# Centring the first row tile on ScalarE, and a 128-column tile of zeros for the warm-up products

## The chip, the cores and the metric

The kernel runs on one core of a Trainium2 chip. The metric is the device time of one execution in microseconds (us); five executions give a median. The profile shows one execution of its own, from the first to the last instruction (the span). Engines are named as the profile names them: PE is TensorE, PEld its weight loads, DVE is VectorE, ACT is ScalarE, POOL is GpSimd, and SP is the engine that issues most of the DMAs.

## The reference

S = 2048 tokens, D = 512 features, F = 1792; everything is bfloat16.

```python
def _layernorm(x, axis=-1, eps=1e-5):
    m = jnp.mean(x, axis=axis, keepdims=True)
    v = jnp.var(x, axis=axis, keepdims=True)
    return (x - m) / jnp.sqrt(v + eps)

def reference(x, w1, w2, w3, w4):
    h = _gelu(_layernorm(x, axis=-1) @ w1)
    # four quarters of the features of h are shifted along S by +1, -1, +2, -2 tokens
    hs = jnp.concatenate([g0, g1, g2, g3], axis=-1) @ w2
    x1 = x + hs
    h2 = _gelu(_layernorm(x1, axis=-1) @ w3) @ w4
    return x1 + h2
```

## The kernel before

The tokens are cut into 16 row tiles of 128 tokens. In layer 1 a tile is normalised in rows (tokens on partitions), transposed to features on partitions (`xnT`), multiplied with w1 and passed through gelu into `hT` ("up1"). "mix" multiplies the shifted `hT` with w2 and DVE adds x, which gives x1. Layer 2 normalises x1 (tile numbers q = 16 to 31), multiplies with w3 and applies gelu ("up2"), and "down" multiplies with w4; DVE adds x1 and the result is stored.

The order of the PE work is written out by hand in `SCRIPT`:

```python
warm:10 sa:0 sb:0 ty:1 ra:0 rb:0 ty:2 up1:1 th:0 up1:2 mix:0 ty:3 ty:5 mix:1 ty:4 up1:3-4 ty:16 mix:2 ty:17
```

`warm:10` is ten products of zeros. `sa`/`sb` are the transposes on PE of the left and the right half of tile 0 (two 128x128 transposes each, L487), and `ty:1` the four transposes of tile 1. `ra`/`rb` are the two halves of tile 0's product with w1 (two 128x512 products each, L525). Tile 0 alone (`NAT`, `SPLIT`) takes another way than the other tiles: it is only centred before its transpose, in two halves of 256 columns, its product comes out in rows, and the gelu (L566) multiplies with 1/std on the way, `rstd0`. `th:0` then turns its result (L591), and DVE copies it into `hT` (L601). Later tiles go through DMA transposes from SP.

All other instructions are placed by a planner (`Program.order`, `place`). It takes a guessed duration `dur` for each operation and a due time that comes from the PE order, runs a list schedule, and so fixes the order on each engine's queue. A changed duration or engine can therefore reorder other operations; the queues themselves run strictly in that order. `emit` puts waits where data demand them. The order of the loads is fixed by `LOADS`: SP issues x1, x2, w1a, w1b, x3, x4-5, w2a, w2b and so on, and ACT issues x0.

The steps of tile 0 that matter here are these. ACT computes the mean with `sum0`, a Copy whose accumulator goes to `mv` (L393), and the sum of squares with `ssq0` (L398). DVE makes the variance, `msq0` and `vpe0` (L406, L410). POOL raises it to the power -1/2 (`rstd0`, L421) and also centres the two halves (`norm0_0` and `norm0_1`, L432). After each transposed half, a copy out of PSUM brings it into `xnT` (L495): ACT does the left half (`ev0_0`) and DVE the right half (`ev0_1`). Tile 1's transposed half goes out in the same way, left by ACT (`ev1act`) and right by DVE (`ev1dve`).

Of the kernel before, what the change touches and what calls it, by code (L numbers as in the profile page):

```python
# [6 lines left out]
P = 128  # L7
ACT_F = mybir.ActivationFunctionType
# [249 lines left out]
        return out  # L258

GROUPS = {1: (1, 1, 1, 1, 2, 1, 4, 2, 2, 1), 2: (2, 4, 4, 2, 4)}  # L260
NORM = {0: "pool", 3: "act", 7: "pool", 8: "act", 9: "pool", 10: "pool", 11: "pool", 12: "pool", 14: "act", 15: "act", 16: "pool", 18: "act", 19: "act", 24: "pool", 25: "act", 26: "pool", 27: "pool", 29: "pool", 30: "pool", 31: "act"}
EVAC = {0: "both", 1: "both", 2: "both", 4: "both", 8: "both", 9: "dve", 10: "dve", 11: "dve", 12: "dve", 13: "dve", 14: "dve", 16: "dve", 17: "dve", 19: "both", 20: "both", 21: "both", 22: "both", 23: "both", 24: "dve", 25: "both", 27: "both", 29: "both", 30: "both", 31: "both"}
STAT_ACT = (0, 7, 9, 12, 13, 15, 18, 21, 25, 29, 30)
TAIL = (256, 128, 128)
# [16 lines left out]
def bass_standalone__mixer_s_mlp__prompt_kernel(nc, x, w1, w2, w3, w4, out):  # L281
# [14 lines left out]
    with ExitStack() as es:  # L296
# [21 lines left out]
        neghalf = sb("neghalf", [P, 1], F32)  # L318
        eps_c = sb("eps_c", [P, 1], F32)
        warm = sb("warm", [P, 1], F32)  # L320
        zeros = sb("zeros", [P, 512], BF16)
        y_ps = es.enter_context(nc.psum_tensor("y_ps", [P, NPAIR, 1024], F32))
        o_ps = es.enter_context(nc.psum_tensor("o_ps", [P, NOB, 512], F32))
        o_bf = o_ps[:, :, :].bitcast(BF16)
# [19 lines left out]


        def consts():
            pg.add("dve", "zeros", lambda e: e.memset(zeros[:], 0.0), writes=[(("zeros",), 0)], dur=300)
            pg.add("pool", "ident0", lambda e: e.memset(ident[:], 0.0), writes=[(("ident",), 0)], dur=200)
            pg.add("pool", "ident1",
                   lambda e: e.affine_select(out=ident[:], in_=ident[:], compare_op=ALU.not_equal, fill=1.0,  # L350
                                             base=0, pattern=[[-1, P]], channel_multiplier=1),
                   reads=[(("ident",), 0)], writes=[(("ident",), 1)], dur=300)
            pg.add("pool", "trip0", lambda e: e.memset(st9[:, :, 6:8], 0.0), writes=[(("trip", 0), 0)], dur=90)
            pg.add("pool", "trip1", lambda e: e.memset(st9[:, :, 8:9], D * LN_EPS), writes=[(("trip", 1), 0)], dur=80)
            pg.add("pool", "epsc", lambda e: e.memset(eps_c[:], LN_EPS), writes=[(("eps",), 0)], dur=70)
            pg.add("pool", "neghalf", lambda e: e.memset(neghalf[:], -0.5), writes=[(("neghalf",), 0)], dur=70)
            pg.add("pool", "pad0", lambda e: e.memset(hT[:, :, 0:2], 0.0), writes=[(("hpad", 0), 0)], dur=100)
            pg.add("pool", "pad1", lambda e: e.memset(hT[:, :, HTW - 2 : HTW], 0.0),
                   writes=[(("hpad", 1), 0)], dur=100)
# [24 lines left out]
        def ln(layer, t):  # L384
            q = t if layer == 1 else NT + t
            src = x_sb[:, t, :] if layer == 1 else x1_sb[:, t, :]
            rs = [(("x", t), 0)] if layer == 1 else [(("x1", t), 0)]
            col = lambda a: a[:, q : q + 1]
            if q in STAT_ACT:
                if layer == 1:  # L390
                    b, v = next_junk()
                    pg.add("act", f"sum{q}",
                           (lambda d: (lambda e: e.activation(d, src, ACT_F.Copy, scale=1.0 / D,  # L393
                                                              accum_out=mv[:, q, 0:1])))(junk[:, b, :]),
                           reads=rs, writes=[(("mv", q), 0), (("junk", b), v)], dur=610)
                b, v = next_junk()
                pg.add("act", f"ssq{q}",
                       (lambda d: (lambda e: e.activation(d, src, ACT_F.Square, accum_out=sums[:, q, 1:2])))(  # L398
                           junk[:, b, :]),
                       reads=rs, writes=[(("ssq", q), 0), (("junk", b), v)], dur=610)  # L400
                if layer == 2:
                    pg.add("dve", f"mean{q}",
                           lambda e: e.tensor_scalar(mv[:, q, 0:1], sums[:, q, 0:1], 1.0 / D, None, ALU.mult),
                           reads=[(("sum", q), 0)], writes=[(("mv", q), 0)], dur=75)
                pg.add("dve", f"msq{q}",
                       lambda e: e.tensor_scalar(mv[:, q, 1:2], mv[:, q, 0:1], mv[:, q, 0:1], LN_EPS, ALU.mult,  # L406
                                                 ALU.subtract),
                       reads=[(("mv", q), 0)], writes=[(("msq", q), 0)], dur=130)
                pg.add("dve", f"vpe{q}",
                       lambda e: e.scalar_tensor_tensor(col(vpe), sums[:, q, 1:2], 1.0 / D, mv[:, q, 1:2], ALU.mult,  # L410
                                                        ALU.subtract),
                       reads=[(("ssq", q), 0), (("msq", q), 0)], writes=[(("vpe", q), 0)], dur=130)
            else:
                pg.add("dve", f"bnst{q}", lambda e: e.bn_stats(st9[:, q, 0:6], src),  # L414
                       reads=rs, writes=[(("st", q), 0)], dur=605)
                pg.add("dve", f"bnag{q}", lambda e: e.bn_aggr(mv[:, q, :], st9[:, q, :]),  # L416
                       reads=[(("st", q), 0), (("trip", 0), 0), (("trip", 1), 0)],
                       writes=[(("mv", q), 0), (("vpe", q), 0)], dur=75)
# [1 line left out]
            pg.add("pool", f"rstd{q}",  # L420
                   lambda e: e.tensor_tensor(col(rstd), var, neghalf[:], ALU.pow),  # L421
                   reads=[(("vpe", q), 0), (("neghalf",), 0)], writes=[(("rstd", q), 0)], dur=470)
            how = NORM.get(q, "dve")
            dst = xn_buf[:, slot(q), :]
            if q in NAT:

                assert how != "act"
                if t in SPLIT:
                    for hh in (0, 1):
                        cs = slice(hh * D // 2, (hh + 1) * D // 2)  # L430
                        pg.add(how, f"norm{q}_{hh}",
                               (lambda a, b: (lambda e: e.tensor_scalar(a, b, mv[:, q, 0:1], None, ALU.subtract)))(  # L432
                                   dst[:, cs], src[:, cs]),
                               reads=rs + [(("mv", q), 0)], writes=[(("xn", slot(q), hh), q)],
                               dur=195 if how == "dve" else 400)
                    return
                pg.add(how, f"norm{q}",
                       lambda e: e.tensor_scalar(dst, src, mv[:, q, 0:1], None, ALU.subtract),
                       reads=rs + [(("mv", q), 0)], writes=[(("xn", slot(q), hh), q) for hh in (0, 1)], dur=330 if how == "dve" else 760)
            elif how == "dve":  # L440
                pg.add("dve", f"norm{q}",
                       lambda e: e.tensor_scalar(dst, src, mv[:, q, 0:1], rstd[:, q : q + 1], ALU.subtract, ALU.mult),  # L442
                       reads=rs + [(("mv", q), 0), (("rstd", q), 0)], writes=[(("xn", slot(q), hh), q) for hh in (0, 1)], dur=330)
            else:
                eng = NMR.get(q, "dve")
                pg.add(eng, f"nmr{q}",
                       lambda e: e.tensor_scalar(nmr[:, q : q + 1], mv[:, q, 0:1], rstd[:, q : q + 1], -1.0,  # L447
                                                 ALU.mult, ALU.mult),
                       reads=[(("mv", q), 0), (("rstd", q), 0)], writes=[(("nmr", q), 0)], dur=130 if eng == "dve" else 280)
                if how == "act":  # L450
                    f = lambda e: e.activation(dst, src, ACT_F.Identity, bias=nmr[:, q : q + 1],  # L451
                                               scale=rstd[:, q : q + 1])
                else:
                    f = lambda e: e.tensor_scalar(dst, src, rstd[:, q : q + 1], nmr[:, q : q + 1], ALU.mult, ALU.add)  # L454
                pg.add(how, f"norm{q}", f, reads=rs + [(("nmr", q), 0), (("rstd", q), 0)],
                       writes=[(("xn", slot(q), hh), q) for hh in (0, 1)], dur=710 if how == "act" else 760)
# [253 lines left out]

        def warm_pe(n):
            b, v = next_bank()

            def f(e):
                for _ in range(n):
                    ins = e.matmul(o_ps[:, b, :], zeros[:, 0:P], zeros[:], start=True, stop=True)  # L716
                return ins

            nwarm[0] += 1
            pg.add("pe", f"warm{nwarm[0]}", f, reads=[(("zeros",), 0)], writes=[(("o", b), v)],  # L720
                   dur=min(n, 7) * 427 + max(0, n - 7) * 216)
            next_bank()
# [145 lines left out]
```

## Time and profile before

| | us |
|---|---|
| median of 5 runs | 135.95 (135.87 to 136.23) |
| the profiled execution, whole | 135.9 |
| its span | 134.6 |
| PE busy in it | 130.8 (97%) |
| DVE, ACT, POOL busy | 50.4, 57.4, 31.5 |
| ten warm-up products on PE (L716), start and length | 0.63, 4.44 |
| POOL's two centring instructions (L432), start and length together | 3.76, 1.82 |

The 1.3 us between the span and the time lie before the first and after the last instruction. PE carries nearly the whole chain that ended last (94%), so a change of another engine's work counts only where PE waits. A line of the timeline gives the start and the length of a merged group in us, the engine (a q behind the name is its queue of DMA issues), the source line, the operation with the tiles out and in, and in brackets how long the engine was idle before and what ended that.

### The profile page before, as it was taken

The numbers are of one execution on the slowest core, as the hardware profiler recorded it, in microseconds if no ns is written. First come the engines' busy times: TensorE is split into PE (matmuls) and PEld (weight loads), VectorE is DVE, ScalarE is ACT, GpSimd is POOL, SyncE is SP. The second block draws the span as 40 slices with busy tenths as digits, with TensorE's granted clock in tenths as the row PEclk, the third lists the DMA queues.
The fourth block names the chain that finished last, engine by engine and source line by source line (L and its number), as shares of the span: only waits on it lengthen the run. The fifth ranks groups of instructions, "written<-read, shape, count | busy, mean of one in ns | idle before, by whom it ended". The sixth has DMA issues, their size and how long they took to land.

```text
span 134.6 us, 2004 instructions
## 1 busy us (share of the span) xinstructions
PE 130.8 (97%) x777; PEld 71.6 (53%) x790; DVE 50.4 (37%) x134; ACT 57.4 (43%) x90; POOL 31.5 (23%) x70
## 2 busy tenths in 40 slices
PE   8899999999999999999999999999999999999994
PEld 3377687644656444479444444444444444444463
DVE  4589976856178930070061004232222200012222
ACT  6379349989534275547315554000000155520000
POOL 3944548893102860006010001100000000000000
DMA  5999998645543134100311000211111100001112
GB/s 159 285 366 405 350 300 214 111 84 117 115 82 81 33 72 92 39 0 3 80 39 39 0 0 0 73 44 42 41 39 61 56 0 0 0 5 39 39 39 78
DMA packets 21289, 12.19 MB, mean 91 GB/s; under 512 B 13856, under 2 KB 20768, under 8 KB 21280
## 3 DMA queue, kind: packets, MB, share of 16 engines
q1 hardware_dynamic: 20704, 11.80, 33.1%
q10 hardware_dynamic: 576, 0.26, 0.7%
q8 instruction: 6, 0.10, 0.3%
q14 instruction: 3, 0.02, 0.1%
HBM read 6.82 MB, written 2.10 MB: 66 GB/s over the span
## 4 chain that ended last, share of the span: by engine, by line
PE 94%; DMA 2%; POOL 1%; issue 1%; DVE 1%; SPq 0%
PE y_ps L623 46%; PE o_ps L692 36%; PE o_ps L663 10%; DMA x_sb<-in_x_dram 2%; PE y_ps L487 1%; POOL xn_buf L432 1%; PE y_ps L525 1%; DVE st L414 1%; DVE o_sb L700 0%; PE o_ps L591 0%; DVE mv L416 0%; POOL rstd L421 0%; SPq L853 0%
## 5 line engine op out<-in xcount | busy, mean ns | idle before, releaser
L623 PE MATMUL y_ps<-xnT,w_sb 128*128 128x512 bf16 (+2 forms) x421 | 63.4, 308 | 0.2
L623 PEld LDWEIGHTS y_ps<-xnT,w_sb 128*128 128x128 bf16 x424 | 38.3, 98 | 24.9
L638 ACT ACTIVATE h2T<-y_ps 128x1024 bf16<-128x1024 f32 (+1 forms) x29 | 28.6, 993 | 48.8 <-PE y_ps L623 48.6
L692 PE MATMUL o_ps<-w_sb,h2T 128*128 128x512 bf16 (+2 forms) x247 | 48.6, 355 | 0.3
L692 PEld LDWEIGHTS o_ps<-w_sb,h2T 128*128 128x128 bf16 x252 | 23.5, 98 | 24.7
L700 DVE TENSOR_TENSOR o_sb<-o_ps,x_sb 128x512 bf16<-128x512 f32 (+2 forms) x18 | 11.4, 631 | 46.9 <-PE o_ps L692 46.9
L421 POOL TENSOR_TENSOR rstd<-mv,neghalf 128x1 f32<-128x1 f32 x21 | 11.5, 549 | 22.6 <-DVE mv L416 14.0
L663 PE MATMUL o_ps<-w_sb,hT 128*128 128x512 bf16 x59 | 14.9, 379 | 0.4 <-issue 0.2
L414 DVE BATCH_NORM_STATS2 st<-x_sb 128x6 f32<-128x512 bf16 x21 | 14.1, 678 | 3.0 <-DMA x_sb<-in_x_dram 2.8
L421 POOL TENSOR_TENSOR rstd<-vpe,neghalf 128x1 f32<-128x1 f32 x11 | 6.0, 546 | 28.5 <-DVE vpe L410 28.5
L670 DVE SCALAR_TENSOR_TENSOR x_sb<-o_ps,x_sb 128x512 bf16<-128x512 f32 x5 | 3.4, 686 | 19.1 <-PE o_ps L663 19.0
L638 ACT ACTIVATE hT<-y_ps 128x512 bf16<-128x512 f32 (+1 forms) x10 | 8.0, 805 | 5.3 <-PE y_ps L623 5.2
L663 PEld LDWEIGHTS o_ps<-w_sb,hT 128*128 128x128 bf16 x64 | 6.0, 98 | 5.8
L674 DVE TENSOR_TENSOR x_sb<-o_ps,x_sb 128x512 bf16<-128x512 f32 x11 | 7.5, 683 | 4.0 <-PE o_ps L663 3.8
L454 POOL TENSOR_SCALAR xn_buf<-x_sb,rstd,nmr 128x512 bf16<-128x512 bf16 x11 | 8.4, 764 | 0.8 <-DVE nmr L447 0.4
L398 ACT ACTIVATE junk<-x_sb 128x512 bf16<-128x512 bf16 x11 | 6.8, 623 | 2.2 <-DVE x_sb L670 2.2
L451 ACT ACTIVATE xn_buf<-x_sb,nmr,rstd 128x512 bf16<-128x512 bf16 x8 | 6.3, 806 | 1.3 <-POOL nmr L447 1.3
L442 DVE TENSOR_SCALAR xn_buf<-x_sb,mv,rstd 128x512 bf16<-128x512 bf16 x12 | 5.5, 456 | 2.8 <-POOL rstd L421 2.6
L716 PE MATMUL o_ps<-zeros 128*128 128x512 bf16 x10 | 4.4, 631 | 0.6 <-POOLq L853 0.6
L393 ACT ACTIVATE junk<-x_sb 128x512 bf16<-128x512 bf16 x6 | 3.7, 624 | 0.5 <-DMA x_sb<-in_x_dram 0.5
L416 DVE BATCH_NORM_AGGREGATE mv<-st 128x2 f32<-128x9 f32 x21 | 3.8, 189 | 0.3
L447 POOL TENSOR_SCALAR nmr<-mv,rstd 128x1 f32<-128x1 f32 x13 | 3.4, 263 | 0.7
(34 smaller groups left out, 29.0 us busy)
## 6 DMA issues: line engine op xcount, KB each, us to landing
out_dram<-o_sb SPq DMA_DIRECT2D x15, 128.0 KB, 1.7
w_sb<-in_w_dram SPq DMA_DIRECT2D x1, 1792.0 KB, 9.9
w_sb<-in_w_dram SPq DMA_DIRECT2D x2, 896.0 KB, 12.4
w_sb<-in_w_dram SPq DMA_DIRECT2D x4, 256.0 KB, 4.8
x_sb<-in_x_dram SPq DMA_DIRECT2D x3, 256.0 KB, 5.7
x_sb<-in_x_dram SPq DMA_DIRECT2D x2, 384.0 KB, 9.6
x_sb<-in_x_dram SPq DMA_DIRECT2D x3, 128.0 KB, 2.4
xnT<-xn_buf SPq DMA_TRANSPOSE x24, 2.5
```

The costliest lines, as they stand in the source:

```text
L398: (lambda d: (lambda e: e.activation(d, src, ACT_F.Square, accum_out=sums[:, q, 1:2])))(junk[:, b, :]),
L414: pg.add("dve", f"bnst{q}", lambda e: e.bn_stats(st9[:, q, 0:6], src), reads=rs, writes=[(("st", q), 0)], dur=605)
L421: lambda e: e.tensor_tensor(col(rstd), var, neghalf[:], ALU.pow),
L442: lambda e: e.tensor_scalar(dst, src, mv[:, q, 0:1], rstd[:, q : q + 1], ALU.subtract, ALU.mult),
L451: f = lambda e: e.activation(dst, src, ACT_F.Identity, bias=nmr[:, q : q + 1], scale=rstd[:, q : q + 1])
L454: f = lambda e: e.tensor_scalar(dst, src, rstd[:, q : q + 1], nmr[:, q : q + 1], ALU.mult, ALU.add)
L623: ins = e.matmul(y_ps[:, p, W * i : W * (i + 1)], wsb[:, dc, P * fc : P * (fc + 1)], src[:, dc, P * t0 : P * t0 + W], start=(dc == 0), sto ...
L638: (lambda d, s: (lambda e: e.activation(d, s, ACT_F.Gelu_apprx_tanh)))(dst, ysrc),
L663: ins = e.matmul(dst, hT[:, j, c0 : c0 + P], w2_sb[:, j, :], start=(j == 0), stop=(j == DC - 1))
L674: f = lambda e: e.tensor_tensor(x1_sb[:, t, :], dst, x_sb[:, t, :], ALU.add)
L692: ins = e.matmul(dst, h2T[:, fc, P * t : P * (t + 1)], w4_sb[:, fc, cs], start=(fc == 0), stop=(fc == FC - 1))
L700: (lambda d, c: (lambda e: e.tensor_tensor(o_sb[:, oi, c], d, x1_sb[:, t, c], ALU.add)))(dst, cs),
```

## The change

Tile 0 is centred by ACT with the Identity function and a bias. For that, `sum0` now scales by -1/D, so the accumulator leaves the negated mean in `mv`. `msq0` squares it, so the variance is computed as before. The two POOL instructions are gone. The planner's durations for these operations change, and with them the order on some queues. The tile of zeros has 128 columns in place of 512, and each warm-up product reads it four times, through a step of zero, as its 512 moving columns.

```diff
-NORM = {0: "pool", 3: "act", ...
+NORM = {0: "act", 3: "act", ...
...
-        zeros = sb("zeros", [P, 512], BF16)
+        zeros = sb("zeros", [P, P], BF16)
...
-            pg.add("dve", "zeros", lambda e: e.memset(zeros[:], 0.0), writes=[(("zeros",), 0)], dur=300)
+            pg.add("dve", "zeros", lambda e: e.memset(zeros[:], 0.0), writes=[(("zeros",), 0)], dur=110)
...
+            how = NORM.get(q, "dve")
+            sign = -1.0 if q in NAT and how == "act" else 1.0
...
-                           (lambda d: (lambda e: e.activation(d, src, ACT_F.Copy, scale=1.0 / D,
+                           (lambda d: (lambda e: e.activation(d, src, ACT_F.Copy, scale=sign / D,
...
+                def center(a, b):
+                    if how == "act":
+                        return lambda e: e.activation(a, b, ACT_F.Identity, bias=mv[:, q, 0:1])
+                    return lambda e: e.tensor_scalar(a, b, mv[:, q, 0:1], None, ALU.subtract)
+
                 if t in SPLIT:
                     for hh in (0, 1):
                         cs = slice(hh * D // 2, (hh + 1) * D // 2)
-                        pg.add(how, f"norm{q}_{hh}",
-                               (lambda a, b: (lambda e: e.tensor_scalar(a, b, mv[:, q, 0:1], None, ALU.subtract)))(
-                                   dst[:, cs], src[:, cs]),
+                        pg.add(how, f"norm{q}_{hh}", center(dst[:, cs], src[:, cs]),
                                reads=rs + [(("mv", q), 0)], writes=[(("xn", slot(q), hh), q)],
-                               dur=195 if how == "dve" else 400)
+                               dur={"dve": 195, "act": 430, "pool": 900}[how])
...
+            rows = zeros[:].unsqueeze(1).to_broadcast([P, 4, P])
...
-                    ins = e.matmul(o_ps[:, b, :], zeros[:, 0:P], zeros[:], start=True, stop=True)
+                    ins = e.matmul(o_ps[:, b, :], zeros[:], rows, start=True, stop=True)
```

More of the change, by code (lines that the diff above doesn't have):

```diff
@@ L260 @@
 GROUPS = {1: (1, 1, 1, 1, 2, 1, 4, 2, 2, 1), 2: (2, 4, 4, 2, 4)}
-NORM = {0: "pool", 3: "act", 7: "pool", 8: "act", 9: "pool", 10: "pool", 11: "pool", 12: "pool", 14: "act", 15: "act", 16: "pool", 18: "act", 19: "act", 24: "pool", 25: "act", 26: "pool", 27: "pool", 29: "pool", 30: "pool", 31: "act"}
+NORM = {0: "act", 3: "act", 7: "pool", 8: "act", 9: "pool", 10: "pool", 11: "pool", 12: "pool", 14: "act", 15: "act", 16: "pool", 18: "act", 19: "act", 24: "pool", 25: "act", 26: "pool", 27: "pool", 29: "pool", 30: "pool", 31: "act"}
 EVAC = {0: "both", 1: "both", 2: "both", 4: "both", 8: "both", 9: "dve", 10: "dve", 11: "dve", 12: "dve", 13: "dve", 14: "dve", 16: "dve", 17: "dve", 19: "both", 20: "both", 21: "both", 22: "both", 23: "both", 24: "dve", 25: "both", 27: "both", 29: "both", 30: "both", 31: "both"}
@@ L422, in ln @@
                    reads=[(("vpe", q), 0), (("neghalf",), 0)], writes=[(("rstd", q), 0)], dur=470)
-            how = NORM.get(q, "dve")
             dst = xn_buf[:, slot(q), :]
             if q in NAT:
-                assert how != "act"
+                assert how != "act" or q in STAT_ACT
+                def center(a, b):
+                    if how == "act":
+                        return lambda e: e.activation(a, b, ACT_F.Identity, bias=mv[:, q, 0:1])
+                    return lambda e: e.tensor_scalar(a, b, mv[:, q, 0:1], None, ALU.subtract)
                 if t in SPLIT:
@@ L430, in ln @@
                         cs = slice(hh * D // 2, (hh + 1) * D // 2)
-                        pg.add(how, f"norm{q}_{hh}",
-                               (lambda a, b: (lambda e: e.tensor_scalar(a, b, mv[:, q, 0:1], None, ALU.subtract)))(
-                                   dst[:, cs], src[:, cs]),
+                        pg.add(how, f"norm{q}_{hh}", center(dst[:, cs], src[:, cs]),
                                reads=rs + [(("mv", q), 0)], writes=[(("xn", slot(q), hh), q)],
-                               dur=195 if how == "dve" else 400)
+                               dur={"dve": 195, "act": 430, "pool": 900}[how])
                     return
-                pg.add(how, f"norm{q}",
-                       lambda e: e.tensor_scalar(dst, src, mv[:, q, 0:1], None, ALU.subtract),
-                       reads=rs + [(("mv", q), 0)], writes=[(("xn", slot(q), hh), q) for hh in (0, 1)], dur=330 if how == "dve" else 760)
+                pg.add(how, f"norm{q}", center(dst, src), reads=rs + [(("mv", q), 0)],
+                       writes=[(("xn", slot(q), hh), q) for hh in (0, 1)], dur={"dve": 330, "act": 650, "pool": 1800}[how])
             elif how == "dve":
```

## The prediction

> **What bounds the kernel now.** I read the page's engine shares first, then the chain in order of time, then the timeline of the first 12 us, and last the DMA issues, cut into windows so narrow that one load stands alone. The chain's start:
>
> ```profile
> 2.20 0.70 DVE st L414
> ...
> 3.76 1.83 POOL xn_buf L432 x2
> 5.59 0.05 issue
> 5.64 0.51 PE y_ps L487 x6
> 6.15 0.86 PE y_ps L525 x4
> 7.01 0.22 PE y_ps L487 x4
> 7.23 0.89 PE y_ps L623 x16
> 8.13 0.22 PE o_ps L591 x4
> 8.35 0.92 PE y_ps L623 x16
> ```
>
> GpSimd's two centring instructions hold PE until 5.64, and from there the chain is PE to the end. It looks as if all time cut before 5.64 were won. But a chain names one releaser per step; others may be nearly as late. The timeline says who:
>
> ```profile
> 7.05 0.70 DVE L414 BATCH_NORM_STATS2 st<-x_sb 128x6 f32<-128x512 bf16 x1 [0.27 <-DMA x_sb<-in_x_dram]
> ...
> 8.52 0.41 DVE L601 COPY hT<-o_ps 128x512 bf16<-128x512 bf16 x1
> 8.76 0.27 POOL L447 TENSOR_SCALAR nmr<-mv,rstd 128x1 f32<-128x1 f32 x1
> ...
> 9.12 0.81 ACT L451 ACTIVATE xn_buf<-x_sb,nmr,rstd 128x512 bf16<-128x512 bf16 x1 [0.36 <-POOL nmr L447]
> 9.21 0.56 PEld L663 LDWEIGHTS o_ps<-w_sb,hT 128*128 128x128 bf16 x4
> ...
> 9.84 0.57 ACT L638 ACTIVATE hT<-y_ps 128x512 bf16<-128x512 f32 x1
> ...
> 10.49 0.58 PEld L663 LDWEIGHTS o_ps<-w_sb,hT 128*128 128x128 bf16 x4
> ...
> 11.02 0.41 DVE L442 TENSOR_SCALAR xn_buf<-x_sb,mv,rstd 128x512 bf16<-128x512 bf16 x1
> ...
> 11.48 0.23 PEld L487 LDWEIGHTS y_ps<-ident,xn_buf 128*128 128x128 bf16 x4 [0.40 <-DVE xn_buf L442]
> ```
>
> and the two loads behind them, each from its own window (size, us from issue to landing):
>
> ```profile
> x_sb<-in_x_dram SPq DMA_DIRECT2D x1, 128.0 KB, 4.9
> ```
> ```profile
> w_sb<-in_w_dram SPq DMA_DIRECT2D x1, 256.0 KB, 5.7
> ```
>
> The first is x3: issued at 2.08, landed at about 7.0; DVE's statistics of tile 3 start at 7.05. The second is w2b, the second half of w2: issued at about 3.48 (the second of two issues that fill 2.97 to 3.95), landed at about 9.18; mix 0 needs it, and its first weight load is at 9.21. So three gates stand between 5.64 and the dense stretch, none of which starts at tile 0:
> - mix 0 at 9.21: w2b.
> - mix 1 at 10.49: the gelu of 9.84, done at 10.41. It queues on ACT behind the normalising of tile 3 (9.12 to 9.93), which waits for POOL's nmr of tile 3 (done 9.03), which goes back to x3.
> - tile 4's transposes at 11.48: DVE's normalising of tile 4, done at 11.43, at the end of a DVE queue that is full from 7.05 on (statistics of tiles 3, 5 and 4 with what lies between). It starts with x3 too.
>
> The arithmetic agrees. From 5.64 to the end of tile 4's transposes (11.48 plus 0.05 and 4 x 0.056, near 11.7) PE has work of 2 + 4 + 4 + 4 + 8 + 4 = 26 transposes at 0.056, 32 products of 128 columns at 0.056 and 12 of 512 at 0.216: 5.8 us in 6.1. PE was late by its own work and held at these gates within 0.1 to 0.3 us. The start was balanced, and only one of the arms gets shorter.
>
> **The change, part by part.**
>
> *Zeros.* The fill took 0.27 for 256 four-byte columns (0.30 to 0.57); a quarter of the columns takes 0.07 to 0.11. PE's first product at 0.63 is put down to two releasers, the fill and a POOL semaphore. If the fill decides, PE starts at 0.47; if not, at 0.63. I take 0.47.
>
> *Warm-up products.* Weight loads 0.427 apart (0.62, 1.03, 1.46 ...): ten make 4.27, so they end at 4.74, before at 4.87 to 4.9. No row shows a product that reads one tile four times. The same count of columns streams, so I take 0.427. Below it nothing speaks for a gain; above, even 0.49 apiece would end at 5.4, still ahead of 5.64.
>
> *POOL loses 2 x 0.92 us.* What stood behind it moves up: rstd of tile 2 from 5.55 to about 4.5.
>
> *ACT gains two instructions* of 256 columns with a pointer as bias. Nearest rows: 0.38 for a copy of 256 columns without a pointer, 0.62 for 512 without, 0.81 for 512 with two, so 0.09 for a pointer: 0.47 each (bounds 0.38 and 0.56). They wait for the mean, read out at 3.14 to 3.32, and run from 3.40 to about 4.25; POOL finished at 5.59. Behind them on ACT the planner puts `ev0_0` and only then `ssq0` (0.61 + 0.18), which now waits behind PE's transposes. So the sum of squares ends not at 3.93 but after 6.
>
> *The new start.* PE reaches tile 0's transposes at 4.74 and finds both halves and tile 1 ready (DVE's normalising of tile 1 ended at 4.37): eight in a row, to about 5.25. `ev0_0` runs 5.08 to 5.46, `ev0_1` about 5.25 to 5.53. w1a landed at 4.8, w1b at about 5.47. Tile 0's product runs from 5.50 to 6.36, before 5.98 to 6.85. That is 0.5 us earlier.
>
> *What is late next.* `ssq0` 5.37 to 6.15, `vpe0` on DVE to 6.35 (tile 1's `ev1dve` queues behind it, to about 6.6), `rstd0` on POOL 6.4 to 6.95, and the gelu of tile 0, which waits for it, at 7.0 (before 7.11). `ev1act` ends at about 6.5, so up1 of tile 1 starts at 6.65 (before 7.07). The 0.5 has shrunk to 0.1 on ACT's arm. Then PE turns tile 0's result at 7.8 and runs up1 of tile 2 from about 8.1 to 9.0.
>
> *At the gates.* mix 0 still waits for w2b: 9.2. DVE waits for x3 at 7.05 as before (the order of its queue from there to 20 us is unchanged), so L601 stays at 8.52 behind the statistics of tile 5, nmr of tile 3 at 8.76, mix 1 at 10.49, tile 4 at 11.48. What is left: mix 0 up to 0.04 earlier, and with it the x1 addition of tile 0, behind which DVE normalises tile 4: 0.05 at most.
>
> *Moved elsewhere.* Some small DVE instructions near 21 and 27 us swap places, the longest delay 0.15 on a DVE that waits for PE or POOL there. On SP the store of the first finished tile, before at 29.33 (0.58 of issue), moves behind eight DMA transposes, to about 40. These come up to 0.6 earlier, where PE did not wait for them; its o_sb slot is used again after 60 us. Nothing.
>
> Sum: the profiled 135.9 (134.6 of span, 1.3 around it) less 0.05; the median, 135.95, is 0.05 above the profiled run. 135.95 - 0.05 = 135.9.
>
> [...] In the trace the first transpose takes 257 ns and the others 219, and weight loads fall from 151 (zeros) over 135 to 98: PE comes to full speed at about 4.9, some 4.2 us after its first product. [...] By the trace, warm-up and switch move together and nothing is lost. [...]
>
> **The rivals.**
>
> [...] Chance 0.15. A smaller relative, `rstd0` late because `ssq0` is: it would take a gelu start after 7.4 against my 7.0, included with 0.05.
>
> *Faster: the gates give way.* If w2b and x3 land earlier in most runs than in the profiled one, the 0.5 passes as far as they allow: 135.95 - 0.3 to 0.5, about 135.55. For it: landings in one execution are one sample. Against: neither load's issue nor what shares its queue is touched, and five runs lie within 0.36. Chance 0.2.
>
> *It doesn't do what it says.* If PE's start stays at 0.63, the transposes start at 4.9, and the gates stand as they are: also 135.9. That belongs to the forecast.
>
> **How the numbers follow.** Forecast of no change 0.6, faster 0.2, slower 0.2 (0.15 + 0.05). A measurement of this kernel can tell about 0.2% from no change, 0.27 us, so 135.68 to 136.22 is "same". The forecast's own range is 135.75 to 136.15. To leave out no more than 2 in 10 the range takes in half of each side: 135.55 to 136.5.
>
> **What would show it.** Right: products of zeros from about 0.47; ACT's L431 at 3.4 with 0.47 each; tile 0's product near 5.5; the gelu of tile 0 near 7.0, released by POOL; a new PE wait of some 0.2 before mix 0 at about 9.2; mix 1 at 10.5 and tile 4's transposes at 11.5 as before. Wrong: tile 4's transposes at 11.2 or earlier (faster), or products of 512 columns still 0.43 apart after 5.5 (the clock).

## The result and the profile after

The changed kernel takes 135.56 us in the median of 25 executions (135.04 to 135.86), the kernel before 136.01 (46 executions). The ratio is 0.9968, with a 95% interval of 0.9961 to 0.9975: 0.43 us faster, where the forecast was 0.05. A few executions of either kernel take 137 to 138 us; the ratios leave out most of these but not all, so medians are given beside them, and the profile of experiment 1 below is of such an execution.

The profile of the changed kernel does not show the gain. Its span is 134.7, before 134.6; that execution took 136.02, longer than any of the 25. Its timeline (start, length, engine, line, operation, and in brackets the idle time before and what ended it):

```profile
0.45 4.44 PE L720 MATMUL o_ps<-zeros 128*128 128x512 bf16 x10 [0.45 <-DVE zeros L347]
...
3.60 0.91 ACT L431 ACTIVATE xn_buf<-x_sb,mv 128x256 bf16<-128x256 bf16 x2
...
5.56 1.02 PE L528 MATMUL y_ps<-w_sb,xnT 128*128 128x512 bf16 x4 [0.23 <-ACT xnT L498]
...
5.95 0.14 PEld L528 LDWEIGHTS y_ps<-w_sb,xnT 128*128 128x128 bf16 x2 [0.29 <-DMA w_sb<-in_w_dram]
...
6.41 0.69 DVE L416 BATCH_NORM_STATS2 st<-x_sb 128x6 f32<-128x512 bf16 x1
...
6.96 0.69 ACT L569 ACTIVATE hn<-y_ps,rstd 128x512 bf16<-128x512 f32 x1 [0.66 <-POOL rstd L423]
...
7.93 0.69 DVE L416 BATCH_NORM_STATS2 st<-x_sb 128x6 f32<-128x512 bf16 x1 [0.54 <-DMA x_sb<-in_x_dram]
...
9.40 0.56 PEld L666 LDWEIGHTS o_ps<-w_sb,hT 128*128 128x128 bf16 x4 [0.46 <-issue]
...
11.56 0.25 PEld L490 LDWEIGHTS y_ps<-ident,xn_buf 128*128 128x128 bf16 x4 [0.29 <-DVE xn_buf L445]
```

and the load of w2's second half in it (size, us from issue to landing):

```profile
w_sb<-in_w_dram SPq DMA_DIRECT2D x1, 256.0 KB, 5.8
```

The same two steps of tile 0 before, its product and its gelu:

```profile
5.98 1.03 PE L525 MATMUL y_ps<-w_sb,xnT 128*128 128x512 bf16 x4
...
7.11 0.69 ACT L566 ACTIVATE hn<-y_ps,rstd 128x512 bf16<-128x512 f32 x1 [0.55 <-PE y_ps L525]
```

The start is as it was worked out: PE at 0.45, ACT's two centring instructions 0.46 each, tile 0's product at 5.56 (before 5.98), its gelu at 6.96 behind POOL's rstd. Then the gates close, though not all the ones that were forecast: tile 3's statistics run at 6.41 without waiting for x3, but DVE then waits 0.54 for x4-5, and mix 0 loads its weights only at 9.40. The row names no load; w2's second half (issued near 3.5) landed at about 9.3, after the copy L604 (8.95) and PE's last product before mix 0, so the load is taken to be what held it. Tile 4's transposes come at 11.56, before at 11.48. By this one profile the forecast of no change holds. By the 25 executions it doesn't.

A second profile of the same kernel (experiment 11, an execution of 135.61) shows another early stretch:

```profile
6.51 0.68 DVE L416 BATCH_NORM_STATS2 st<-x_sb 128x6 f32<-128x512 bf16 x1
...
8.23 0.42 DVE L604 COPY hT<-o_ps 128x512 bf16<-128x512 bf16 x1 [0.18 <-PE o_ps L594]
...
8.99 0.59 PEld L666 LDWEIGHTS o_ps<-w_sb,hT 128*128 128x128 bf16 x4
...
11.21 0.23 PEld L490 LDWEIGHTS y_ps<-ident,xn_buf 128*128 128x128 bf16 x4 [0.32 <-DVE xn_buf L445]
```
```profile
w_sb<-in_w_dram SPq DMA_DIRECT2D x1, 256.0 KB, 5.2
```

Here w2 has landed at about 8.7, mix 0 follows PE's own work, the copy L604 is released by PE and not by a DVE queue filled late, and tile 4's transposes come 0.35 earlier. The span is 134.3.

### The profile page after: what moved, and what is told of

Read it like the earlier page. It is cut to its first block, busy times and chain, and to the rows that moved or that the text cites. A ratio compares the mean times of both kernels' runs of the same rounds, so it can differ in the third digit from the quotient of the medians.

```text
span 134.7 us, 2003 instructions
## 1 busy us (share of the span) xinstructions
PE 131.0 (97%) x777; PEld 71.7 (53%) x790; DVE 50.4 (37%) x134; ACT 58.5 (43%) x92; POOL 29.8 (22%) x68
## 4 chain that ended last, share of the span: by engine, by line
PE 91%; DMA 4%; DVE 1%; issue 1%; SPq 0%
PE y_ps L626 44%; PE o_ps L695 36%; PE o_ps L666 10%; DMA x_sb<-in_x_dram 4%; DVE st L416 1%; PE y_ps L490 1%; SPq L368 0%; DVE hT L604 0%; DVE o_sb L703 0%; DVE mv L418 0%
## 5 line engine op out<-in xcount | busy, mean ns | idle before, releaser
L423 POOL TENSOR_TENSOR rstd<-mv,neghalf 128x1 f32<-128x1 f32 x21 | 11.5, 549 | 23.2 <-DVE mv L418 14.3
```

## The experiments

Theory A was formed after the result: the start's gain is real, and how much of it passes depends on when w1b, w2, x3 and x4-5 land, which differs from execution to execution. Rivals: B, the gain comes from the queues reordered after 20 us; C, it comes from the earlier warm-up; D, the gain is the same whatever the loads do.

The kernel before ran beside each batch: its median was 135.99 us beside experiments 1 to 4, 136.05 beside 5 to 8 and 136.13 beside 9 to 11. In 5 to 11 the ratio comes out 0.0005 to 0.002 lower than the quotient of the medians; for the changed kernel itself, in experiment 11, it is 0.995, and the medians give 0.9968 as at first. Small differences of the ratios are therefore read with the medians. In the cuts below, `behind(pg, a, b)` moves operation `a` in its queue to the place right behind `b`, and `...` stands for lines left out.

**1. ACT centring alone** (zeros stay 512 columns wide).

```diff
-        zeros = sb("zeros", [P, P], BF16)
+        zeros = sb("zeros", [P, 512], BF16)
...
-            rows = zeros[:].unsqueeze(1).to_broadcast([P, 4, P])
...
-                    ins = e.matmul(o_ps[:, b, :], zeros[:], rows, start=True, stop=True)
+                    ins = e.matmul(o_ps[:, b, :], zeros[:, 0:P], zeros[:], start=True, stop=True)
```

> ACT centres tile 0 as in the changed kernel, but the tile of zeros keeps its 512 columns, so PE starts at 0.63 and the warm-up products end at about 4.87 in place of 4.7. All queues are ordered as in the changed kernel. Theory A (the start's gain passes wherever the loads of w2, x3 and x4-5 land early enough): tile 0's transposes 0.15 to 0.2 later than in the changed kernel, so some 0.1 to 0.2 less gain: ratio to before 0.9975 to 0.9985. Theory B (the gain comes from the changed order of queues after 20 us): 0.9968 as with the whole change. Theory C (the gain comes from the earlier start of the warm-up and of PE's full clock): 1.000.

Measured: 0.998 (0.9967 to 0.9994), median 135.81, 0.18 below before. The value is A's, though the interval just reaches B's 0.9968. The profile, of an execution of 137.54 us, shows PE waiting for w2 at mix 0:

```profile
10.96 0.56 PEld L666 LDWEIGHTS o_ps<-w_sb,hT 128*128 128x128 bf16 x4 [2.57 <-DMA w_sb<-in_w_dram]
```

**2. The narrow zeros alone**, with POOL centring.

```diff
-        zeros = sb("zeros", [P, 512], BF16)
+        zeros = sb("zeros", [P, P], BF16)
...
+            rows = zeros[:].unsqueeze(1).to_broadcast([P, 4, P])
...
-                    ins = e.matmul(o_ps[:, b, :], zeros[:, 0:P], zeros[:], start=True, stop=True)
+                    ins = e.matmul(o_ps[:, b, :], zeros[:], rows, start=True, stop=True)
```

> POOL centres tile 0 as before and all queues are ordered as before; only the tile of zeros is 128 columns wide and read four times by each warm-up product. Theories A and B: POOL's second half still ends at 5.59 and holds PE, so ratio 1.000 (within 0.1%). Theory C: 0.9968, all of the gain.

Measured: 0.9999 (0.9984 to 1.0013). C falls. In its profile POOL still holds PE, and later than in the profile of before (5.63):

```profile
5.79 0.34 PEld L487 LDWEIGHTS y_ps<-ident,xn_buf 128*128 128x128 bf16 x6 [0.79 <-POOL xn_buf L432]
```

**3. The sum of squares first** on ACT.

```diff
         pg.order()
+        behind(pg, "ssq0", "norm0_1")
```

> The changed kernel with one instruction moved on ACT: the sum of squares of tile 0 runs ahead of the copy of its left transposed half (as before the change), every other queue unchanged. The sum of squares then ends near 5.0 to 5.2 in place of 6.0, rstd of tile 0 about 0.2 to 0.3 earlier (it still queues behind tile 2's normalising on DVE), the gelu of tile 0 near 6.7 in place of 6.96; the left half's copy may be up to 0.15 later. Theory A: if ACT's arm still limits in executions with early loads, 0.1 to 0.3 us faster than the changed kernel, ratio to before 0.995 to 0.996; if the loads limit, 0.9968. Theory B: 0.9968.

Measured: 0.9968 (0.9957 to 0.9979), the same as the changed kernel. The gelu began at 6.84, and PE released it in place of POOL, but in this execution w1's second half came last: the right half of tile 0's product waited for it.

```profile
6.12 0.11 PEld L528 LDWEIGHTS y_ps<-w_sb,xnT 128*128 128x128 bf16 x2 [0.35 <-DMA w_sb<-in_w_dram]
```

So in this profile a shorter arm of ACT alone gains nothing while w1b is as late, and the median, 135.56, says the same of the executions.

**4. The new start with the old queues** from tile 3 on.

```diff
-                        pg.add(how, f"norm{q}_{hh}", center(dst[:, cs], src[:, cs]),
+                        pg.add("pool", f"norm{q}_{hh}", center(dst[:, cs], src[:, cs]),
...
-                               dur={"dve": 195, "act": 430, "pool": 900}[how])
+                               dur=400)
...
         pg.order()
+        for op in pg.seq:
+            if op.name in ("norm0_0", "norm0_1"):
+                op.eng = "act"
+        behind(pg, "norm0_0", "sum0")
+        behind(pg, "norm0_1", "norm0_0")
+        behind(pg, "ssq0", "ev0_0")
+        behind(pg, "vpe0", "norm2")
+        behind(pg, "rstd0", "vpe0")
```

The planner again sees POOL centring and the old durations (that of the fill with zeros is among the lines left out), so it orders the later queues as before.

> The whole change at the start (ACT centres, narrow zeros), but all queues from tile 3 on are ordered as before the change: the store of the first tile at its old place on SP, the small DVE instructions near 21 and 27 us in their old order. Theory A: the order later counts for nothing, ratio 0.9968 as with the whole change. Theory B: the gain is gone, ratio 1.000.

Measured: 0.9972 (0.996 to 0.9984), median 135.61. B falls: the old order of the later queues keeps the gain. Its profile is of an execution with early loads (w2b at about 8.3) and with PE at full speed early (the ten products of zeros take 4.21 in place of 4.44); tile 4's transposes start at 10.87, and the span is 134.0.

**5 and 6. The loads out of the way**, on both kernels.

```diff
+            if layer == 1 and t in (3, 4, 5):
+                src = x_sb[:, 2, :]
...
-                        ins = e.matmul(y_ps[:, p, 0:D], xnT[:, dc, P * t : P * (t + 1)], w1_sb[:, dc, :],
+                        ins = e.matmul(y_ps[:, p, 0:D], xnT[:, dc, P * t : P * (t + 1)], w1_sb[:, dc % 2, :],
...
+            wsb = w1_sb if t in (0, 1) else w2_sb
...
```

The lines left out at the end replace the waits for the loads in the same way.

> The kernel before with the loads taken out of the way of the first 12 us: the right half of tile 0's product uses the first half of w1 again, mix 0 and mix 1 use w1 in place of w2, and tiles 3 to 5 of layer 1 take their statistics and their normalised rows from tile 2 of x (so these parts of the result are other numbers). All queues keep their order. Theory A (the start's gain is cut by late loads): before is late by POOL's centring and its own PE work and only now and then by a load, so little changes: ratio to before 0.997 to 1.000. Theory D (the loads limit before as much as the changed kernel, and the 0.43 comes out whatever the loads do): the same 0.2 to 0.4 us for both kernels, ratio 0.997 to 0.9985.

> The changed kernel with the same loads taken out of the way (the right half of tile 0's product with the first half of w1, mix 0 and mix 1 with w1, tiles 3 to 5 of layer 1 normalised from tile 2 of x; those parts of the result are other numbers). All queues keep their order. Theory A: the whole 0.5 to 0.6 us of the earlier start passes, and what the loads had held back comes free as well: 0.1 to 0.4 us faster than the changed kernel, ratio to before 0.993 to 0.996, and more than 0.43 us between this and the kernel before with the loads out of the way. Theory D: 0.43 us between the two, as with the loads in the way.

Measured: before with the loads out of the way 0.9988 (0.9973 to 1.0002), median 136.04; the changed kernel 0.9938 (0.9914 to 0.9963), median 135.42. The kernel before does not care about the loads: 22 executions, and 0.01 from before beside it in the median. That the changed one does, as A has it, is not shown. The medians of the two lie 0.62 us apart in place of 0.43, but that rests on six executions of the changed kernel, three from 135.11 to 135.24 and three from 135.61 to 135.66, and the widths of the intervals do not exclude D's 0.43. The profile is of one of the fast three, and its tile 4, at 10.81, is hardly earlier than the 10.87 of experiment 4, which had all loads in the way. The tile 4 lines of the two profiles, before and changed in this order:

```profile
11.63 0.23 PEld L489 LDWEIGHTS y_ps<-ident,xn_buf 128*128 128x128 bf16 x4 [0.42 <-DVE xn_buf L444]
```
```profile
10.81 0.23 PEld L492 LDWEIGHTS y_ps<-ident,xn_buf 128*128 128x128 bf16 x4 [0.38 <-DVE xn_buf L447]
```

The first, without any gate, is later than before's 11.48 with its gates. The reason lies in POOL's queue. The centring stands there behind rstd of tile 1, which waits for x1's statistics:

```profile
3.47 0.56 POOL L423 TENSOR_TENSOR rstd<-mv,neghalf 128x1 f32<-128x1 f32 x1 [1.78 <-DVE mv L418]
4.02 1.82 POOL L434 TENSOR_SCALAR xn_buf<-x_sb,mv 128x256 bf16<-128x256 bf16 x2
```

In the profile of before, rstd began at 3.21; here at 3.47, in experiments 2 and 7 at 3.36 and 3.33. So PE's second half of tile 0 came at 5.79 to 5.95 in these three, and 5.64 was an early one. The gelu of tile 0 was later as well: 7.27, 7.38 and 7.42 in experiments 2, 5 and 7, against 7.11.

**7 and 8. w1's second half issued by ACT**, on both kernels.

```diff
+        w1b = next(op for op in pg.seq if op.name == "dma_w1b")
+        w1b.eng = w1b.queue = "act"
+        behind(pg, "dma_w1b", "dma_x0")
```

> The kernel before, but the load of w1's second half is issued by ACT behind x0 (at about 0.6) in place of SP (1.47), so that every later load of SP is issued 0.47 us earlier; ACT's table load starts 0.4 us later, which ends at about 2.3, before x0 lands. All other queues keep their order. Theory A: before is held by POOL's centring until 5.64 and then by its own work; ratio 0.998 to 1.000. Theory D: a gain as large as on the changed kernel.

> The changed kernel with w1's second half issued by ACT behind x0, so that every later load of SP is issued 0.47 us earlier. All other queues keep their order. Theory A: the loads of w1b, w2b and x3 to x5 land 0.2 to 0.5 earlier, wait less for, so 0.1 to 0.3 us faster than the changed kernel: ratio to before 0.9945 to 0.996. If the loads are limited by what the memory delivers and not by their issue, nothing: 0.9968. If the first tiles of x land later because w1b now competes with them, slower than the changed kernel: above 0.998.

Measured: before 0.9997 (0.9986 to 1.0007), median 136.08; the changed kernel 0.9954 (0.9938 to 0.997), median 135.63. Earlier loads give before nothing. Nor is a gain shown on the changed kernel: the ratio is better than 0.9968, as A expected, but the intervals overlap, and the median is 0.42 below before's, as without the edit. In its profile no wait for w1's second half is left, and the gelu of tile 0 is what is late:

```profile
7.07 0.69 ACT L569 ACTIVATE hn<-y_ps,rstd 128x512 bf16<-128x512 f32 x1 [0.66 <-POOL rstd L423]
```

**9 and 10. ACT's arm shortened as well, and w1's first half ahead of x2**; 11 is the changed kernel once more beside them. Both keep w1's second half on ACT; the last line is in experiment 10 only.

```diff
+        behind(pg, "ssq0", "norm0_1")
+        behind(pg, "vpe0", "ev0_1")
+        behind(pg, "dma_x2", "dma_w1a")
```

> The changed kernel with w1's second half issued by ACT behind x0, and with tile 0's sum of squares (ACT) and variance (DVE) ahead of the copies and of tile 2's normalising, so that rstd of tile 0 no longer holds its gelu. In the profile of the kernel with the load alone moved, that gelu began at 7.07, released by POOL's rstd, while its product had ended at about 6.55. Theory A (with the loads earlier, ACT's arm is what is late next): the gelu 0.3 us earlier, tile 4's transposes near 10.9 to 11.0, 0.1 to 0.3 us faster than with the load alone moved: ratio to before 0.993 to 0.9945. If loads still decide: as with the load alone moved, about 0.9955.

> As the kernel before this one in the list (w1b issued by ACT, sum of squares and variance of tile 0 early), and w1's first half issued by SP ahead of x2, at about 0.53 in place of 0.99; x2 comes 0.45 later. The left half of tile 0's product waited for w1's first half in two profiles (5.41 and 5.66). Theory A: it starts up to 0.2 earlier; tile 1's and tile 2's normalising may be up to 0.4 later, where there is slack for tile 2: ratio 0.992 to 0.9945. If the two halves of w1 slow down x1 or x0, it is slower than its neighbour: above 0.9945.

> The changed kernel itself once more, beside the others on the same chip and with a second profile. Theory A: 0.9968 as measured; in the profile, w2's second half lands near 8.3 to 8.9 (as in most profiles so far) in place of 9.3, mix 0 loads its weights at 8.7 to 9.0 and tile 4's transposes come at 11.0 to 11.2 in place of 11.56; span less the start of these transposes is 123.1 us as in all other profiles. Rival: the profile again shows 11.5 and a span of 134.7, and the gain is to be found after tile 4.

Measured side by side: 0.9939 (0.9915 to 0.9962), median 135.50, with ACT's arm shortened; 1.0002 (0.998 to 1.0025), median 136.37, with w1's first half early; 0.995 (0.9922 to 0.9977), median 135.70, for the changed kernel itself, 0.43 below before as at first. In the first, PE releases the gelu:

```profile
6.78 0.69 ACT L569 ACTIVATE hn<-y_ps,rstd 128x512 bf16<-128x512 f32 x1 [0.90 <-PE y_ps L528]
```

Its median is 0.2 below the changed kernel beside it, but the intervals overlap: that it beats the changed kernel is likely and not shown.

The second missed: its median is 0.67 above the changed kernel's and 0.24 above before's. x2, issued at 1.00 instead of 0.5, landed at about 5.4 instead of about 2.9, and not 0.45 later. In experiment 9, which differs by this one move alone, DVE's statistics of tile 2 began at 3.29 and waited for no load. Both halves of w1 (issued at 0.54 and 0.62) now went ahead of x2; how much of the delay is due to each is not shown. On DVE's queue the statistics of tile 2 stand ahead of the normalising of tile 1, so tile 1 was late too (6.03, in experiment 9 4.05), and PE waited 1.32 for it:

```profile
5.42 0.69 DVE L416 BATCH_NORM_STATS2 st<-x_sb 128x6 f32<-128x512 bf16 x1 [2.03 <-DMA x_sb<-in_x_dram]
...
6.03 0.40 DVE L445 TENSOR_SCALAR xn_buf<-x_sb,mv,rstd 128x512 bf16<-128x512 bf16 x1
...
6.48 0.40 PE L490 MATMUL y_ps<-ident,xn_buf 128*128 128x128 bf16 x4 [1.32 <-DVE xn_buf L445]
```

**Where the time is decided.** From all the profiles: when w2b landed (its issue plus the time to landing), when mix 0 loaded its first weights, when tile 4's transposes loaded theirs, and the span less that.

| | w2b | mix 0 | tile 4 | span | rest |
|---|---|---|---|---|---|
| before | 9.2 | 9.21 | 11.48 | 134.6 | 123.1 |
| 2 zeros alone | 8.9 | 9.21 | 11.52 | 134.6 | 123.1 |
| 5 before, no loads | 8.4 | 9.32 | 11.63 | 134.7 | 123.1 |
| 7 before, w1b by ACT | 7.8 | 9.37 | 11.68 | 134.8 | 123.1 |
| changed | 9.3 | 9.40 | 11.56 | 134.7 | 123.1 |
| 11 changed again | 8.7 | 8.99 | 11.21 | 134.3 | 123.1 |
| 1 ACT alone | 10.9 | 10.96 | 13.11 | 136.2 | 123.1 |
| 3 sum of squares first | 8.6 | 8.78 | 11.10 | 134.2 | 123.1 |
| 4 old later queues | 8.3 | 8.65 | 10.87 | 134.0 | 123.1 |
| 6 changed, no loads | 8.7 | 8.53 | 10.81 | 133.9 | 123.1 |
| 8 w1b by ACT | 8.0 | 9.01 | 11.23 | 134.3 | 123.1 |
| 9 and ACT's arm | 7.5 | 8.72 | 11.04 | 134.1 | 123.1 |
| 10 w1a ahead of x2 | 8.2 | 9.87 | 12.20 | 135.3 | 123.1 |

The last column is the same to 0.1 in all thirteen. All that these kernels gain or lose in these executions is decided before tile 4's transposes; what follows takes the same time, whatever the order of the queues.

Loads are not all that differs ahead of it. Experiment 4 and the changed kernel in experiment 11 have the same start (PE at 0.43), but PE comes to full speed at different times. Tile 0's and tile 1's transposes and the gelu of tile 0, in experiment 4 and then in 11:

```profile
4.47 0.62 PE L490 MATMUL y_ps<-ident,xn_buf 128*128 128x128 bf16 x8
...
6.71 0.69 ACT L569 ACTIVATE hn<-y_ps,rstd 128x512 bf16<-128x512 f32 x1 [0.66 <-PE y_ps L490]
```
```profile
4.67 1.06 PE L490 MATMUL y_ps<-ident,xn_buf 128*128 128x128 bf16 x8
...
7.05 0.69 ACT L569 ACTIVATE hn<-y_ps,rstd 128x512 bf16<-128x512 f32 x1 [0.66 <-POOL rstd L423]
```

In 11 the transposes run at half speed (0.107 us from one to the next in place of 0.056). The copy `ev0_0` on ACT begins at 5.13 in place of 4.78, and behind it the sum of squares, rstd and the gelu are 0.34 to 0.35 later; so are mix 0 (8.99 and 8.65) and tile 4's transposes (11.21 and 10.87). w1b was later too and held PE to 6.10 in place of 5.85, so 0.25 of this could have come from the load alone; no run separates the two. Experiment 8, with w1b out of the way and the same slow transposes, came to 7.07 for the gelu and 11.23 for tile 4. What is late next in the changed kernel is thus a load in its first profile and ACT's arm in its second; how often each is the last is not known.

The gain itself can be followed in two executions near the medians: experiment 2, which is before but for the zeros (135.95 us), and the changed kernel in experiment 11 (135.61). In neither does anyone wait for w2, x3 or x4-5. The gelu of tile 0 comes at 7.27 and 7.05, mix 0 at 9.21 and 8.99, tile 4's transposes at 11.52 and 11.21.

## Why the prediction was right and where it was wrong

- *The range and the forecast.* The median of 135.56 is 0.01 above the low end of the stated range and 0.34 below the forecast of 135.9. The range reached down to 135.55 only because half of the rival "the gates give way" was taken into it. That the median lies inside is luck; the mechanism behind the forecast was wrong.
- *POOL's two instructions hold PE until 5.64, and the start becomes 0.5 earlier.* Right in kind, and the 0.4 at tile 0's product was seen (5.98 to 5.56). It may be more in most executions: in the profiles of experiments 2, 5 and 7 the centring on POOL began 0.1 to 0.3 later than in the profile of before. The 0.62 between experiments 5 and 6 points the same way, with six executions on one side.
- *Zeros and warm-up products.* Right: PE at 0.45 (0.47 forecast), products 0.427 apart through the repeated tile, and alone worth nothing (0.9999). Together with ACT's centring, the wider zeros in experiment 1 cost some 0.1% by the ratios, within their intervals.
- *ACT's cost.* Right: 0.46 each against 0.47. It began at 3.60 and not 3.40, because x0 landed 0.25 later (`sum0`, which waits for it, began at 2.85, before at 2.60).
- *What is late next: ACT's arm, gelu at 7.0.* Right: 6.96 and 7.05, released by POOL. But "the 0.5 has shrunk to 0.1" set this against a gelu of 7.11 from an early execution of before. Against the 7.27 to 7.42 of experiments 2, 5 and 7, ACT's arm gains 0.2 to 0.5. Not seen was w1's second half: I took its landing of 5.47 from one profile; it held the right half of tile 0's product to 5.69 to 6.12 in profiles of the changed kernel and its variants.
- *"At the gates. mix 0 still waits for w2b: 9.2. DVE waits for x3 at 7.05 as before."* This is the step that failed. In the changed kernel's first profile it holds to 0.2 us for mix 0, mix 1 and tile 4, but already not for x3, on which no one waited. Over executions it doesn't hold: w2b landed anywhere from 8.3 to 9.3 in the eight profiles that leave its issue alone, experiment 1's aside, tile 3's statistics ran at 6.51 without a wait in the second profile, and tile 4's transposes, at 11.21 in place of 11.5, moved with tile 0. I treated landings of one execution, with w2b and x3 late, as properties of the kernel. The term "what is left: 0.05 at most" measured 0.43.
- *"The start was balanced, and only one of the arms gets shorter."* Wrong for the same reason: experiments 5 and 7 show that before gains nothing from open gates or earlier loads (136.04 and 136.08, beside it 136.05), so its loads had slack in the typical execution. In the one profile read, POOL's centring was early and w2b late, which made the arms look equal.
- *Order of later queues: nothing.* Right (experiment 4, and the constant 123.1).
- *The rival "the gates give way", about 135.55.* This is nearest to what happened, at 135.56, with one amendment: in the typical execution the gates did not hold before either. Its counterargument, that neither load's issue is touched, is true and beside the point: a load need not be changed to be earlier than in the one profile read.
- *The clock.* I took "warm-up and switch move together" from the trace; that was wrong. Eight transposes after the ten products took 0.62 (experiment 4), 0.64 (changed), 0.80 (experiment 3) and 1.06 us (experiments 8 and 11), all with PE's start at 0.43 to 0.45: at about full speed in the first two (0.056 us from one to the next), at half speed in the last (0.107). In experiment 1 the switch came within the ten products, which took 3.66 in place of 4.44 (shortest, median and longest in ns, then the first and the last start in us):

```profile
L719 PE MATMUL o_ps<-zeros x10: 379/620/634, 0.6 to 3.9; 128*128 128x512 bf16 x10
```

A product at full speed takes 0.21 less (0.216 against 0.427 apart), so by my estimate nearly four of the ten ran at full speed, and the switch came some 2.7 us after PE's start. In 8 and 11 the last of the transposes, 5.0 us after the start, still ran at half speed. So the switch moved by over 2 us from execution to execution. What sets it off no run shows, and so none shows a ground for the 0.15 that I gave to a slower clock. The runs show tile 0's product beginning at 5.66 to 5.68 even after the slowest of these transposes, its four products at full speed (1.02 to 1.06 for the group), and 25 executions that end at 135.86, far from the 136.5 to which the range reaches on that side.

## What to carry to other kernels

In this kernel a wait that ends in a transfer was a draw, not a constant (w2's second half, issued at 3.5, landed at 8.3 to 9.3 in eight profiles and at 10.9 in a ninth): before a gain is written off against it, read the landing in several profiles, and ask whether the one in hand is early or late. Then find the last place up to which spans differ (here tile 4's transposes, with 123.1 us behind them in every profile), and argue about what lies ahead of that alone. Before a transfer is moved forward, ask whom it passes and who stands behind that: in experiment 10 x2 came 2.5 us later for 0.5 in the queue of issues, and on DVE's queue tile 1's normalising, behind x2's statistics, came at 6.03 in place of 4.05.

## What the runs showed of the hardware that I had not expected

- The load of w2's second half, issued at the same time (3.5) in nine of these profiles, landed 8.3 to 9.3 us after the start in eight of them and at 10.9 in that of 137.54 us, where PE waited 2.6 us for w2 at mix 0. In that one the long execution is a late load: the granted clock was 1.000 as in all other runs.
- Issued 0.5 us later, behind both halves of w1 (experiment 10), x2 landed some 2.5 us later (5.4 against 2.9).
- PE's switch to full speed came from some 2.7 us (estimated above, experiment 1) to more than 5.0 us (experiments 8 and 11) after its first product. Since the centring no longer holds the transposes back, they can fall ahead of the switch, and ACT's arm then starts later (5.13 in experiment 11, 4.78 in experiment 4). The granted clock reads 1.000 in every profile and does not show this; the spacing of the products does.
- A product that reads its 128 columns of zeros four times, through a step of zero, takes the time of one that reads 512 separate columns: ten take 4.44 us in both kernels, 0.427 apart.
